# A DFT along the features as seven block products instead of eight

## The chip, the core and the metric

The kernel runs on one NeuronCore of a Trainium2 chip. A core has TensorE (PE in the profile; PEld is its weight load), VectorE (DVE), ScalarE (ACT), GpSimdE (POOL) and SyncE (SP, which here issues the DMAs). Each engine takes its instructions in the order in which the program lists them, and they wait for each other through semaphores. The metric is the device time of one execution in microseconds (us), the median of several runs.

## The reference

Input x is 2048 rows (tokens) by 512 features, and four sublayers run one after the other: A, B, A, B, each with a residual.

```python
def A(x, Ws_re, Ws_im, Wd_re, Wd_im):        # x is a layernorm of the running sum
    a = x @ Wd_re.T                          # DFT along the 512 features
    b = x @ Wd_im.T
    return Ws_re @ a - Ws_im @ b             # DFT along the 2048 tokens, real part

def B(x, w1, w2, w3, w4):                    # 512 -> 512 -> 512, then 512 -> 1376 -> 512
    x1 = x + shifts(gelu(layernorm(x) @ w1)) @ w2
    return x1 + gelu(layernorm(x1) @ w3) @ w4

x = x + A(layernorm(x)); x = x + B(layernorm(x)); x = x + A(layernorm(x)); x = x + B(layernorm(x))
```

One A and the B behind it are called a layer: layer 0 and layer 1. The kernel forms A the other way round: first both token transforms of the normed x, which give a real part (`re`) and an imaginary part (`im`), then the two feature transforms, which it adds.

## The kernel before, in words

**Precision.** A float32 operand is split in two: its rounded high part, made by ScalarE with a copy, and the low rest, made by VectorE with a subtraction. `mm3` (line 294) then issues three matmuls for one product: high by high, high by low, low by high. PE work is therefore counted in threes.

**Chunks and phases.** An A sublayer goes through four chunks of 512 output tokens. A chunk has two phases. `x_phase` (line 499) has 16 half steps, here called s0 to s15: an even one multiplies into the PSUM pairs PC and PB (12 matmuls of 128x512), an odd one into PA (6 matmuls). `y_phase` (line 528) has 16 half steps of 12 matmuls each, here y0 to y15, into PC with PD and into PB with PA. Behind the y phase VectorE puts the sums together in the tiles `re0`, `re1`, `im0`, `im1` (two 128-row blocks each of re and im), and they are split by `high` (ScalarE, line 449) and `low` (VectorE, line 452).

**Feature transforms.** Those of a chunk c are `hid` calls (line 577). For chunks 0 to 2 they are put into the x phase of the chunk behind, eight calls of 12 matmuls of 128x512 at the half steps that `HAT` (line 39) names, into the two PSUM banks PD, four calls for each half of the chunk's tokens. `add_y` (line 593) then adds PD to the rows held in X0 or X1 and sums the rows in the same instruction. For chunk 3 they follow its y phase by themselves.

**What feeds PE.** Every half step and every `hid` call takes one slot of `ring`, four buffers of 1 MB. The slots are filled in a fixed list of items: SyncE loads the raw matrix into one of the `raw` buffers, `stage_one` (line 228) takes differences on VectorE where an item needs them and makes the high part on ScalarE, `stage_two` (line 252) makes the low part on VectorE. `stream()` (line 283) is called once for each item, before its matmuls. It counts the slot of the item before as given back, and lets `prefetch` (line 270) issue `stage_one` of the item three places ahead and `stage_two` of the item two places ahead. An item X so reuses the slot of the item four places before it, and its filling waits until PE has finished with that item. An even half step has an item of the kind "plain" (ScalarE copies 1024 elements a partition, VectorE subtracts 1024), an odd one of the kind "one" (VectorE subtracts 512, ScalarE copies 512, VectorE subtracts 512), a y half step one of the kind "by1" or "by0" (VectorE 1024, ScalarE 1024, VectorE 1024).

**Order by hand.** `late` maps a half step's number to functions; `run_late(i)` runs them right behind that half step's `stream()`, ahead of its matmuls. Nothing reorders the instructions afterwards, so each engine meets them in the order of the code. `hook(i)` behind it issues loads and stores of rows (`rows`, line 204), by SyncE.

**The rest.** The B sublayer (`by_pairs`, line 752) handles chunks in two pairs. In layer 0 the second pair is a loop of five turns (line 1066), then a tail of 11 steps with work of the next layer in `next_steps` (line 986).

Of the kernel before, what the change touches and what calls it, by code (L numbers as in the profile page):

```python
# [40 lines left out]
HORDER = ((1, 0), (0, 1), (1, 1), (0, 0))  # L41


@with_exitstack
def spectral_mlp_kernel(ctx: ExitStack, tc: tile.TileContext, x, ws, hs, w1, w2, w34, out):
# [8 lines left out]
    junk = const.tile([P, D], mybir.dt.bfloat16, name="junk")  # L54
# [10 lines left out]
    w4d = [dram.tile([P, 2, CH], F32, name=f"w4d{i}") for i in range(NF)]  # L65

# [96 lines left out]
    for layer in range(LAYERS):  # L163
        for c in range(NC):
            if layer == 0 and c == 0:
                for k in range(NP):
                    item("plain", piece(ws[c, k][:, 2:4]))
                    item("plain", piece(ws[c, k][:, 0:2]))
                continue
            for k in range(NP):  # L170
                if c:
# [19 lines left out]
    for n, it in enumerate(items):  # L191
        for i in it[1]:
# [3 lines left out]
    state = {"wide": False, "dma": 0, "one": 0, "two": 0, "use": 0, "made": 0, "done": 0, "limit": 0, "load": w_pieces[0]}  # L196
# [11 lines left out]
    def issue_dma(upto=None):  # L208
        while state["dma"] < (state["load"] if upto is None else upto):
# [4 lines left out]
                if (r < RAW or state["wide"] and i in y_pieces)  # L214
# [12 lines left out]

    def stage_one():
# [8 lines left out]
        slots[n] = dest  # L237
        r = [raws[i] for i in ids]
# [13 lines left out]
    def stage_two():  # L252
        n = state["two"]
        kind, ids, (a, b), _ = items[n]
        dest = slots[n]
# [189 lines left out]
    re0s, re1s, im0s, im1s = (f[:, :, 1] for _, f in (re0, re1, im0, im1))  # L445
    mid = [rr[i // 2][i % 2].rearrange("p t r (h d) -> p (t r h) d", h=2) for i in range(4)]
# [52 lines left out]
    def x_phase(c, hook):  # L499
        h = 0  # L500
        for k in range(NP):
            first, last = k == 0, k == NP - 1
            while c and h < NP and HAT[h] == k:
# [12 lines left out]
            if last:  # L516
                for i in range(2):
                    nc.scalar.copy(im1s[:, i], PC[i])  # L518
# [9 lines left out]
    def y_phase(c, hook):  # L528
        for k, kind in y_order():
            first, last = k == 0, k == NP - 1  # L530
            s = stream()
            if kind == "by1":
                hook(k)
                if k == 1:
                    run_late("y")
                if k == 3:
# [5 lines left out]
                if last:  # L542
# [7 lines left out]
                    high(im0)  # L550
            else:
                if k == NP - 2:
# [6 lines left out]
        for i in range(2):  # L559
            nc.scalar.copy(t[:, 2 + i], PA[i])  # L560
        late.update(
# [190 lines left out]
    def by_pairs(layer, zs, xin, dst):  # L752
# [291 lines left out]
        bg += [lows("t4"), *early]  # L1044
        bk, acc1 = mm4, acc4
# [20 lines left out]
        for p in range(NF // 2):  # L1066
# [19 lines left out]
            for f, h in tiles:  # L1086
# [14 lines left out]
            one()  # L1101

        then = next_steps()
        while bg:
            one()

# [577 lines left out]
    for layer in range(LAYERS):  # L1684
        xin = x if layer == 0 else x2d
        last_layer = last_of(layer)
        state["limit"] = w_items[layer]
        zs = {}
        for c in range(NC):
# [90 lines left out]
            def hook(i):  # L1780
# [8 lines left out]
                if i == (13 if layer == 0 and c else 11):  # L1789
                    state["wide"] = True  # L1790
                if c == 0:
# [19 lines left out]
                if i == 4:  # L1811
# [3 lines left out]
                if i == 9:  # L1815
# [3 lines left out]
                if c == NC - 1 and i == 12:  # L1819
                    for j in (0, 1):  # L1820
                        normed_act(tmp[:, j], xt(j), ln2[j])

            x_phase(c, hook)

            def hook(k):
                if layer == 0:
                    prepare_at(c, 2 * NP + k)
                if layer and c == 0:
                    for step, f in zip((1, 1, 2), (ay_sums, ay_highs, ay_lows)):
                        if k == step:  # L1830
                            f(7)
                if k == 1 and c:
                    rows(X1, x1d, (c - 1) * TC + 2, 2, False)
                if c == NC - 1 and k < 2:
                    for q in (2 * k, 2 * k + 1):
                        turn_one(turned0, q, tmp[:, q])
                    for j in (2, 3)[: 2 - 2 * k]:
                        normed_act(tmp[:, j], xt(j), ln2[j])
                if c == NC - 1 and k == 2:
                    turn_out(turned0)  # L1840
# [3 lines left out]
            y_phase(c, hook)  # L1844
# [85 lines left out]
```

## Time and profile before

| what | value |
|---|---|
| median of 3 runs | 1418.96 us (1418.96 to 1420.74) |
| the profiled execution's own time | 1418.97 us |
| its span, first to last instruction | 1417.2 us |
| PE busy | 1409.0 us (99%) |
| VectorE busy | 1191.3 us (84%) |
| ScalarE busy | 765.5 us (54%) |
| all DMA queues | 316.18 MB, mean 223 GB/s |
| granted TensorE clock | 1.000 |

How to read it: the profile is of one execution, and the time around its span is 1.8 us. Busy time counts an instruction from its start to its end, and neighbours on one engine overlap a little, so what an instruction costs an engine that is full is the distance from one start to the next. A row of the timeline has the start, the duration, engine, line, operation, the tiles written and read, and in brackets the idle time before it and what ended it.

### The profile page before, as it was taken

The page shows a single profiled execution, that of the slowest core. Times are in us where ns is not written, and L with a number is a line of the kernel's source. Part 1 is how long each engine was busy: PE and PEld are TensorE (multiplying, and loading weights), DVE is VectorE, ACT ScalarE, POOL GpSimd, SP SyncE. Part 2 cuts the span into 40 slices and gives each one's busy share as a digit, 9 for nine tenths or more (in the row PEclk, how much of TensorE's full clock was granted, in tenths as well). Part 3 has the DMA queues.
Part 4 walks back from the last instruction along what each step waited for, and adds up shares of the span by engine and source line. Part 5 has one row for each costly group of instructions (what it writes and reads, how often), then busy time and mean ns, then how long its engine had stood idle before and what let it go on. Part 6 is the DMA issues. An engine that isn't in the chain of part 4 may idle for free.

```text
span 1417.2 us, 18479 instructions
## 1 busy us (share of the span) xinstructions
PE 1409.0 (99%) x6669; PEld 1181.8 (83%) x6669; DVE 1191.3 (84%) x1684; ACT 765.5 (54%) x1072; POOL 68.2 (5%) x105
## 2 busy tenths in 40 slices
PE   9999999999999999999999999999999999999998
PEld 8888788888788888988888888888888888899887
DVE  7988998998988789956789979879889788897776
ACT  6664555556566655534555545645555566454351
POOL 2100000000001100000000000000000020000000
PEclk9999999999999999999999999999999999999999
DMA  8978858778774748865556476565587457687864
GB/s 290 306 236 302 268 194 274 241 230 309 255 228 146 253 165 264 257 247 180 195 177 218 136 225 206 166 220 170 193 265 237 134 141 245 188 250 252 297 205 160
DMA packets 158907, 316.18 MB, mean 223 GB/s; under 512 B 10848, under 2 KB 78816, under 8 KB 156896
## 3 DMA queue, kind: packets, MB, share of 16 engines
q1 hardware_dynamic: 158816, 315.01, 67.9%
q8 instruction: 52, 0.85, 0.2%
q14 instruction: 39, 0.32, 0.1%
HBM read 260.70 MB, written 54.26 MB: 222 GB/s over the span
## 4 chain that ended last, share of the span: by engine, by line
PE 94%; DVE 3%; DMA 1%; ACT 1%; issue 1%; SPq 0%; POOL 0%; DVEq 0%; ACTq 0%; POOLq 0%
PE psd L295 10%; PE psd L296 10%; PE psd L297 10%; PE psa L295 8%; PE psa L297 8%; PE psa L296 8%; PE psb L296 7%; PE psb L297 7%; PE psb L295 7%; PE psc L295 6%; PE psc L296 6%; PE psc L297 6%; DMA raw<-in_ws 1%; DVE ring L258 1%; DVE rest L492 0%
## 5 line engine op out<-in xcount | busy, mean ns | idle before, releaser
L241 ACT CAST ring<-raw 128x1024 fp32r<-128x1024 f32 x127 | 132.9, 1052 | 69.4 <-PE psd L297 30.6
L258 DVE TENSOR_TENSOR ring<-raw,ring 128x1024 fp32r<-128x1024 f32 x126 | 153.4, 1220 | 14.3 <-ACT ring L241 14.3
L295 PE MATMUL psd<-ring,rr 128*128 128x512 f32 x208 | 80.9, 389 | 0.0
L296 PE MATMUL psd<-ring,rr 128*128 128x512 f32 x208 | 80.9, 389 | 0.0
L297 PE MATMUL psd<-ring,rr 128*128 128x512 f32 x208 | 80.9, 389 | 0.0
L248 ACT CAST ring<-ring0f 128x1024 fp32r<-128x1024 f32 x28 | 29.5, 1054 | 46.9 <-DVE ring0f L247 46.9
L258 DVE TENSOR_TENSOR ring<-ring1f,ring 128x512 fp32r<-128x512 f32 (+1 forms) x56 | 53.3, 952 | 0.8 <-ACT ring L244 0.7
L346 POOL TENSOR_TENSOR rows<-ve,mhalf 128x4 f32<-128x4 f32 x16 | 18.2, 1136 | 735.2 <-DVE ve L345 735.2
L295 PE MATMUL psc<-ring,ay 128*128 128x512 f32 x128 | 50.0, 391 | 1.6 <-ACT rr11f L518 1.6
L296 PE MATMUL psb<-ring,ay 128*128 128x512 f32 x128 | 50.0, 391 | 1.2 <-DVE ring L258 1.2
L297 PE MATMUL psb<-ring,ay 128*128 128x512 f32 x128 | 49.8, 389 | 0.0
L295 PE MATMUL psb<-ring,ay 128*128 128x512 f32 x128 | 49.8, 389 | 0.0
L296 PE MATMUL psc<-ring,ay 128*128 128x512 f32 x128 | 49.8, 389 | 0.0
L297 PE MATMUL psc<-ring,ay 128*128 128x512 f32 x128 | 49.8, 389 | 0.0
L297 PE MATMUL psa<-ring,ay 128*128 128x512 f32 x126 | 49.0, 389 | 0.0
L295 PE MATMUL psa<-ring,ay 128*128 128x512 f32 x126 | 49.0, 389 | 0.0
L295 PE MATMUL psd<-ring,ay 128*128 128x512 f32 x126 | 49.0, 389 | 0.0
L296 PE MATMUL psd<-ring,ay 128*128 128x512 f32 x126 | 49.0, 389 | 0.0
L296 PE MATMUL psa<-ring,ay 128*128 128x512 f32 x126 | 49.0, 389 | 0.0
L297 PE MATMUL psd<-ring,ay 128*128 128x512 f32 x126 | 49.0, 389 | 0.0
L314 POOL TENSOR_TENSOR rs<-ve,mhalf 128x2 f32<-128x2 f32 (+2 forms) x33 | 28.5, 863 | 412.4 <-DVE nb L313 393.4
L697 DVE TENSOR_TENSOR rg<-gt,rg 128x512 fp32r<-128x512 f32 x32 | 22.1, 690 | 29.6 <-ACT rg L696 29.6
(834 smaller groups left out, 4617.1 us busy)
## 6 DMA issues: line engine op xcount, KB each, us to landing
raw<-in_ws SPq DMA_DIRECT2D x183, 512.0 KB, 5.4
raw<-in_hs SPq DMA_DIRECT2D x56, 512.0 KB, 3.7
w3b<-w3d SPq DMA_DIRECT2D x11, 1792.0 KB, 8.5
w4r<-w4d SPq DMA_DIRECT2D x22, 512.0 KB, 3.5
un<-w4s SPq DMA_DIRECT2D x40, 256.0 KB, 3.7
un<-w4d SPq DMA_DIRECT2D x38, 256.0 KB, 4.4
x1d<-tmp SPq DMA_DIRECT2D x12, 512.0 KB, 6.8
xs<-x1d SPq DMA_DIRECT2D x12, 512.0 KB, 5.2
```

Of the source, the lines that this page charges most:

```text
L241: nc.scalar.copy(dest[:, a:b, 0], r[0][:, a:b])
L248: nc.scalar.copy(dest[:, :, 0], lo)
L258: nc.vector.tensor_tensor(lo, src, hi.bitcast(F32), op=ALU.subtract)
L295: nc.tensor.matmul(o, lh, rh, start=first, stop=False, skip_group_check=more)
L296: nc.tensor.matmul(o, lh, rl, start=False, stop=False, skip_group_check=more)
L297: nc.tensor.matmul(o, ll, rh, start=False, stop=last, skip_group_check=more)
L314: nc.gpsimd.tensor_tensor(rs[:, :n], ve[:, :n], mhalf[:, 0, :n], op=ALU.pow)
L346: nc.gpsimd.tensor_tensor(rs, ve, mhalf[:, :, :2], op=ALU.pow)
L697: nc.vector.tensor_tensor(lo, src, hi.bitcast(F32), op=ALU.subtract)
```

## The change

In layer 1, the feature transforms of chunks 0, 1 and 2 are done by a scheme of seven block products in place of eight (Strassen's, in Winograd's form). The left matrix is the chunk's [re; im], cut into four blocks of 256 tokens by 512: a11 and a21 are re, a12 and a22 are im. The right matrix is the pair of DFT matrices, cut in the same way. There are seven left forms (four blocks and sums of them) and seven right forms. A product (`form_product`) takes 24 matmuls of 128x256, and its sums stay in a PSUM bank, onto which later products are added; a drain adds the bank to a half of X0 or X1 after each.

- **Right forms** are made once, in layer 0's second pair: eight units, each 128 columns of the four blocks (`right_load`: two DMAs; `right_sums`: four subtractions of 128 columns on VectorE and copies of seven on ScalarE; `right_keep`: subtractions of seven on VectorE and two or three DMAs to the DRAM tensor `hfd`). Units 0 to 4 go into the five turns of the loop, 5 to 7 into the tail.
- **In the list of items** a product's item has the kind "ready": one DMA of 1 MB from `hfd` straight into the ring's slot, and no work on ScalarE or VectorE. The eight `hid` items of a chunk go.
- **Left forms** replace the splits of im0, re1, im1, re0: seven ScalarE copies and seven VectorE subtractions of 1024, and five further VectorE sums of 1024. The split of im0 leaves the y phase.
- **Row sums**, which `add_y` gave with the addition, are now four ScalarE activations.
- One of four raw buffers is taken for a left form from y half steps k = 5 until half step 14. Some row loads, stores and transposes of chunk 3 move.

`FORMS` gives, for a half step, the product that goes ahead of it, and `DRAINS`, for a product, the half step whose `run_late` drains it. When P3 and P4 are drained, the rows of X0 and X1 are complete and are summed and squared on ScalarE. With P2 for product 2 and so on, the x phase of chunks 1 to 3 in layer 1 now runs: s0 s1 s2 s3 s4 **P2** s5 s6 **P1** s7 **P5** s8 s9 **P6** s10 **P3** s11 **P7** s12 s13 **P4** s14 s15. Bank PD[1] holds P2, P5, P3 (P3 added onto P5), bank PD[0] holds P1, P6, P7, P4, each added onto the last.

```diff
+FORMS = {5: 2, 7: 1, 8: 5, 10: 6, 11: 3, 12: 7, 14: 4}
+DRAINS = {2: 7, 1: 9, 5: 10, 6: 11, 7: 13, 3: 13, 4: 15}
+RIGHT = (1, 6, 2, 3, 5, 7, 4)
...
-                item("plain", p)
-                item("one", p, span=(0, 1))
+                for i, kind in enumerate(("plain", "one")):
+                    if c and layer and 2 * k + i in FORMS:
+                        item("ready", FORMS[2 * k + i])
+                    item(kind, p, span=(0, 2 - i))
...
     def stage_one():
+        if kind == "ready":
+            to = in_forms(dest).rearrange("p u h w -> p (u h w)")
+            nc.sync.dma_start(to.bitcast(F32), hfd[RIGHT.index(ids[0])].rearrange("p u h w -> p (u h w)"))
+            state["one"] += 1
+            return
...
     def x_phase(c, hook, seven=False):
+            if seven and 2 * k in FORMS:
+                form_product(c - 1, FORMS[2 * k])
-            while c and h < NP and HAT[h] == k:
+            while c and not seven and h < NP and HAT[h] == k:
...
+            if seven and 2 * k + 1 in FORMS:
+                form_product(c - 1, FORMS[2 * k + 1])
             s = stream()
             run_late(2 * k + 1)
...
+    def form_product(c, n):
+        s = in_forms(stream())
+        hi, lo, _ = left_forms[n]
+        bank = PD[n in (2, 5, 3)]
+        new = n in (1, 2, 5)
+        for u in range(4):
+            for q in range(2):
+                v = slice(q * P, (q + 1) * P)
+                first = new and u == 0 and q == 0
+                o = bank[:, q * 2 * P : (q + 1) * 2 * P]
+                mm3(o, hi[:, u, v], lo[:, u, v], s[:, u, 0], s[:, u, 1], first, True, not first)
...
+        late.setdefault(DRAINS[n], []).append(
+            lambda: add(x[:, :, cols], bank.rearrange("p (q w) -> p q w", q=2), x[:, :, cols])
+        )
+        if n in (3, 4):
...
+                (14 if n == 3 else "y", row_sums),
+                (15 if n == 3 else "y2", lambda: squares(known, [x[:, 0], x[:, 1]])),
...
     def y_phase(c, hook, seven=False):
+                    if not seven:
+                        high(im0)
...
+        if seven:
+            late.update(
+                {
+                    1: [lambda: add(im1s, im1s, re1s, ALU.subtract), lambda: add(im1s, im1s, X1)],
+                    2: [left_sum("12-22"), left_high(2)],
+                    3: [left_low(2), lambda: add(re1s, re1s, t[:, 0:2])],
+                    4: [lambda: add(re0s, re0s, t[:, 0:2]), lambda: add(re0s, re0s, t[:, 2:4]), left_high(1)],
+                    5: [left_sum(7), left_sum(5)],
+                    6: [left_low(1), left_high(5)],
+                    7: [left_low(5), left_sum(6), left_high(6)],
+                    8: [left_sum(3), left_low(6), left_high(7)],
+                    9: [left_low(7), left_high(3)],
+                    10: [left_low(3), left_high(4)],
+                    11: [left_low(4)],
+                }
+            )
+            return
...
+                if i == 0:
+                    right_sums(p)
+                else:
+                    right_keep(p)
...
+            if not p:
+                right_keep(p)
+            if p < NF // 2 - 1:
+                right_load(p + 1)
...
+        for n, (f, u) in zip((0, 1, 4, 5, 6, 7, 7, 10, 11), ((right_load, 5), (right_load, 6), (right_sums, 5),
+            (right_keep, 5), (right_sums, 6), (right_keep, 6), (right_load, 7), (right_sums, 7), (right_keep, 7))):
+            then[n].append(do((f, u)))
...
-                if i == 4:
+                if i == (3 if layer else 4):
                     rows(X1, xin, j + 2, 2, True)
                 if i == 5:
                     rows(X0, xin, j, 2, True)
-                if i == 9:
+                if i == (15 if layer else 9):
                     rows(X0, x1d, j, 2, False)
```

More of the change, by code (lines that the diff above doesn't have):

```diff
@@ L53, in spectral_mlp_kernel @@
     mhalf = const.tile([P, 2, TC], F32, name="mhalf")
-    junk = const.tile([P, D], mybir.dt.bfloat16, name="junk")
+    junk32 = const.tile([P, 2, P], F32, name="junk")
+    junk = junk32.rearrange("p a b -> p (a b)").bitcast(mybir.dt.bfloat16)
     nc.gpsimd.memset(mhalf, -0.5)
@@ L65, in spectral_mlp_kernel @@
     w4d = [dram.tile([P, 2, CH], F32, name=f"w4d{i}") for i in range(NF)]
+    hfd = dram.tile([7, P, 4, 2, 2 * P], F32, name="hfd")
     ZW = KD * 2 * CH + 32
@@ L170, in spectral_mlp_kernel @@
             for k in range(NP):
-                if c:
+                if c and not layer:
                     for h in range(NP):
@@ L195, in spectral_mlp_kernel @@
     held = {i: None for i in range(len(raw_at))}
-    state = {"wide": False, "dma": 0, "one": 0, "two": 0, "use": 0, "made": 0, "done": 0, "limit": 0, "load": w_pieces[0]}
+    state = {"wide": False, "kept": 0, "dma": 0, "one": 0, "two": 0, "use": 0, "made": 0, "done": 0, "limit": 0, "load": w_pieces[0]}
     x_left = [(0, 1), (1, 1)] + [(j, 2) for j in range(2, NT, 2)]
@@ L254, in stage_two @@
         kind, ids, (a, b), _ = items[n]
+        if kind == "ready":
+            state["two"] += 1
+            return
         dest = slots[n]
@@ L445, in spectral_mlp_kernel, with name_blocks @@
     re0s, re1s, im0s, im1s = (f[:, :, 1] for _, f in (re0, re1, im0, im1))
+    re_im = [both(f"all{i}", RR + i * 8 * CH, KD, 2, CH) for i in range(2)]
+    apart = re0, re1, im0, im1
+    together = [[t[:, 2 * h : 2 * h + 2] for t in pair] for pair in re_im for h in range(2)]
+    def name_blocks(blocks):
+        nonlocal re0, re1, im0, im1, re0s, re1s, im0s, im1s
+        re0, re1, im0, im1 = blocks
+        re0s, re1s, im0s, im1s = (f[:, :, 1] for _, f in blocks)
     mid = [rr[i // 2][i % 2].rearrange("p t r (h d) -> p (t r h) d", h=2) for i in range(4)]
@@ L497, in run_late, with x_phase @@
                 f()
[L499 removed]
+    def x_phase(c, hook, seven=False):
         h = 0
@@ new lines, in left_high, with left_low, left_sum @@
+    def left_high(n):
+        hi, _, src = left_forms[n]
+        return lambda: nc.scalar.copy(hi, src)
+    def left_low(n):
+        hi, lo, src = left_forms[n]
+        return lambda: nc.vector.tensor_tensor(lo, src, hi.bitcast(F32), op=ALU.subtract)
+    def left_sum(n):
+        f = {i: v[2] for i, v in left_forms.items()}
+        o, a, b, op = {
+            7: (f[7], f[1], f[5], ALU.subtract),
+            6: (f[6], f[4], f[7], ALU.subtract),
+            "12-22": (f[3], f[2], f[4], ALU.subtract),
+            3: (f[3], f[3], f[7], ALU.add),
+            5: (f[5], f[5], f[4], ALU.add),
+        }[n]
+        return lambda: add(o, a, b, op)
@@ L529, in y_phase @@
+    def y_phase(c, hook, seven=False):
         for k, kind in y_order():
@@ L549, in y_phase @@
                         nc.scalar.copy(X1[:, i], PD[i])
-                    high(im0)
+                    if not seven:
+                        high(im0)
             else:
-                if k == NP - 2:
+                if k == NP - 2 and not seven:
                     low(im0)
@@ L1788, in hook @@
                         xp_lows(NP - 1, False)
-                if i == (13 if layer == 0 and c else 11):
+                if i == (13 if c else 11):
                     state["wide"] = True
+                if i == 14:
+                    state["kept"] = 0
+                    if layer and c == NC - 1:
+                        name_blocks(apart)
                 if c == 0:
@@ L1819, in hook @@
                 if c == NC - 1 and i == 12:
-                    for j in (0, 1):
+                    for j in (2, 3) if layer else (0, 1):
                         normed_act(tmp[:, j], xt(j), ln2[j])
-            x_phase(c, hook)
+            x_phase(c, hook, layer and c)
             def hook(k):
```

99 lines of the change are left out of this document (87 added, 12 removed).

## The prediction

> **What bounds the kernel now.** I read the head of the page first, then who PE waited for, then the stretches of layer 1's chunks.
>
> ```profile
> PE 1409.0 (99%) x6669; PEld 1181.8 (83%) x6669; DVE 1191.3 (84%) x1684; ACT 765.5 (54%) x1072; POOL 68.2 (5%) x105
> ```
> ```profile
> PE psc L295 <- ACT rr11f L518: 1.6, 2, 0.8
> PE psd L140 <- POOL ident masks.py:199: 1.4, 1, 1.4
> PE psb L296 <- DVE ring L258: 1.2, 1, 1.2
> ```
> ```profile
> core 0: us, PE busy (x) PEld busy (x) DVE busy (x) ACT busy (x) POOL busy (x), PEclk, DMA share, GB/s
> 895.40:949.80 54.40, 54.40 (x241) 45.05 (x241) 43.30 (x53) 27.26 (x34) 1.21 (x2) 1.00 0.63 201
> 949.80:993.20 43.40, 43.40 (x193) 35.92 (x193) 39.76 (x39) 24.01 (x31) 1.34 (x2) 1.00 0.57 184
> ```
>
> PE never rests for long: its three waits add up to 4.2 us of 1417.2. The last two rows are chunk 2's x and y phase in layer 1: PE busy throughout, VectorE 80% and 92%. So time can only come out by PE work taken away, and VectorE is the engine next in line. The first wait also shows that PE waits for a PSUM bank until its sums have been copied out.
>
> PE's price is the distance between starts:
>
> ```profile
> 884.80 0.39 PE L297 MATMUL psc<-ring,ay 128*128 128x512 f32 x1
> ...
> 895.23 0.39 PE L295 MATMUL psc<-ring,ax 128*128 128x512 f32 x1
> ...
> 1299.74 0.28 PE L295 MATMUL psc<-un,hr 128*128 128x256 f32 x1
> ...
> 1304.95 0.28 PE L296 MATMUL psc<-un,hr 128*128 128x256 f32 x1
> ```
>
> The first two are 46 matmuls apart, the last two 46 as well: 10.43/46 = 0.2267 us for 512 columns, 5.21/46 = 0.1133 for 256. Half the columns cost half the time, though each still loads its weights. An even half step is so 12 x 0.2267 = 2.72 us, an odd one 1.36, a `hid` call 2.72, a product 24 x 0.1133 = 2.72.
>
> **What is removed.** Eight `hid` calls become seven products: 21.76 - 19.04 = 2.72 us a chunk, 8.2 us for three. That is the whole gain to be had, because the other engines' savings end no wait.
>
> [...] The measured distances are exactly 2:1, so no fixed part shows here.
>
> **What is added on VectorE, and when.** These rows are chunk 2's x phase, which begins at 895.23:
>
> ```profile
> 895.43 0.69 DVE L243 TENSOR_TENSOR ring3f<-raw 128x512 f32<-128x512 f32 x1 [1.32 <-PE psa L297]
> 896.04 1.22 DVE L258 TENSOR_TENSOR ring<-raw,ring 128x1024 fp32r<-128x1024 f32 x1
> 897.17 0.68 DVE L258 TENSOR_TENSOR ring<-ring3f,ring 128x512 fp32r<-128x512 f32 x1
> 897.78 1.22 DVE L492 TENSOR_TENSOR rr11f<-rr11f,rr01f 128x1024 f32<-128x1024 f32 x1
> 902.23 0.69 DVE L243 TENSOR_TENSOR ring2f<-raw 128x512 f32<-128x512 f32 x1 [0.59 <-PE psb L297]
> ...
> 926.71 0.69 DVE L243 TENSOR_TENSOR ring1f<-raw 128x512 f32<-128x512 f32 x1 [1.03 <-PE psa L297]
> ```
> ```profile
> L492 DVE TENSOR_TENSOR rest<-rest,psd 128x512 f32<-128x512 f32 x21 | 14.4, 686 | 6.2 <-PE psd L297 4.7 <-issue 1.1
> L450 ACT CAST rr<-rr00f 128x1024 fp32r<-128x1024 f32 x8 | 8.4, 1054 | 20.2 <-DVE rr00f L492 20.2
> ```
>
> Three things. Prices: 1.13 us from start to start for 1024 elements (call it A), 0.61 for 512 (B); a drain reads 512 from PSUM, by the L492 row no dearer, so B. Order: slot fillings, then `late` work, as in the code. And the wait: the subtraction for an odd half step (L243) stands until PE has finished the item four places back. At 902.23 it filled s5's slot, which s2 had: s2 ends at 895.23 + 2 x 2.72 + 1.36 = 902.03, and the row starts 0.20 later. It writes only the half that s2's first six matmuls read, yet waits for the last six. VectorE's queue stands with it.
>
> On average VectorE fits: eight low parts (9.1) and four `add_y` (2.7) go from 43.3; four more low parts (4.5), five sums (5.7) and seven drains (4.3) come, 46 in 51.7. But a product added onto a bank, or opening it anew, waits for the drain of the one before, and the drain sits behind such a wait. Step by step, in us from a product's start:
>
> - **P5** reuses P2's bank, drained at half step 7. Between P1 and P5 VectorE's queue reads: s9's subtraction (it takes P1's slot), s8's low part, form 5's low part, sum 6, drain of P2. It stands until P1 is done at 2.72 + 0.20, then needs B + 3A + B = 4.61: P5 starts at 7.6 with 0.1 for the last end and the semaphore. P1 and s7 are over at 4.08. **PE stands 3.6.**
> - **P7** adds onto P6, drained at step 11. Queue: s13's subtraction (P3's slot), s12's low, form 4's low, drain of P6: 2.92 + B + 2A + B = 6.4, +0.1, against 4.08. **2.4.**
> - **P4** adds onto P7, drained at step 13 behind P3's. Queue: s15's subtraction (s12's slot; s12 ends 5.44 after P7's start), s14's low, two drains: 5.64 + 3B + A = 8.6, +0.1, against 6.8. **1.9.**
> - **P1** needs form 1, a block of re0 and re1, which take three sums first. From the phase's start to form 1's low part the queue holds 3 A and 6 B of slot work, eight sums and two low parts: 13 A + 6 B = 18.4. It begins at 0.2, and it stands up to 0.6 more where form 2's low part waits for its high part (1.05 on ScalarE, by the L450 row, if that one waits for the sum that reads the same tile). Form 1 is ready at 18.7 to 19.3; P1's place is at 17.7. **1.5** (1.0 to 1.6).
> - P2 (form 2 done by 9.5, place 10.9), P6 (drain of P1 6.3 after P5's start, place 6.8) and P3 stand for nothing; cover gone, each costs what VectorE is late.
> - **y0** takes PC and PD. ScalarE has P3's row sums ahead of the copies of PC, and P4's drain is late in VectorE's queue:
>
> ```profile
> L337 ACT ACTIVATE junk<-tmp,rows 128x512 bf16<-128x512 f32 x24 | 17.3, 722 | 5.9 <-DVE rows L335 5.2
> L337 ACT ACTIVATION_READ_ACCUMULATOR junk<-tmp,rows 128x1 f32 x24 | 4.5, 187 | 0.0
> ```
>
> Two row sums take 2 x 0.9 = 1.8 in front of the copies; half is covered by the odd half step s15 (1.36). **0.6** (0 to 1.5).
>
> Sum: 3.6 + 2.4 + 1.9 + 1.5 + 0.6 = 10.0 a chunk; less 2.72 it is +7.3, for three chunks **+21.9**.
>
> **DMAs.** A "ready" item waits on SyncE for the slot, so its 1 MB has the three items between: 2.72 + 1.36 + 2.72 = 6.8 us.
>
> ```profile
> w3b<-w3d SPq DMA_DIRECT2D x6, 1024.0 KB, 5.7
> rt<-xtd SPq DMA_DIRECT2D x2, 1024.0 KB, 10.0
> zd<-turned SPq DMA_DIRECT2D x16, 256.0 KB, 5.8
> ```
>
> At 5.7 it lands in time, at 10.0 it would be 3.2 late. The row nearest in kind is the first (whole rows of 8 KB, the DMA share 0.63), and the stalls above widen the windows of P5, P7 and P4; so nothing, upper bound 2 a chunk. Behind a waiting "ready" SyncE holds the raw loads and the row loads at half steps 3 and 5, which have over 10 us. Moved on SyncE's queue are the store of X0 (half step 9 to 15; X0 is not written again before the next y phase has ended) and, for chunk 3, the store of the transposed rows, from k = 2 of the y phase to k = 5, 10.9 ahead of the load that reads them at k = 7:
>
> ```profile
> zt0f<-zd SPq DMA_DIRECT2D x4, 1024.0 KB, 6.7
> ```
>
> Stores of 5.8 end in time; the load lands 38.1 + 6.7 = 44.8 into the phase, and the first to read it is ScalarE behind the first 24 matmuls that follow the phase's 43.5, at 49. No cost, with 4 us to spare.
>
> **Right forms in layer 0.** A unit adds to VectorE four subtractions of 128 columns and 896 of low part; to SyncE 128 KB loads and stores in runs of 512 bytes.
>
> ```profile
> 640.00:655.00 15.00, 15.00 (x68) 12.43 (x67) 9.47 (x18) 6.65 (x11) 0.89 (x2) 1.00 0.55 197
> 700.00:720.00 20.00, 20.00 (x90) 16.57 (x89) 14.55 (x26) 10.86 (x16) 2.04 (x4) 1.00 0.76 259
> 750.00:760.00 10.00, 10.00 (x46) 8.25 (x45) 10.00 (x11) 7.99 (x11) 0.00 (x0) 1.00 0.73 221
> L492 DVE TENSOR_TENSOR sumaf<-sumaf 128x256 f32<-128x256 f32 x6 | 2.6, 426 | 0.2
> ```
>
> With at most 0.43 for a subtraction and 1.1 for the low parts, a unit is below 2.8 us, nearer 2. A turn of the loop (15 us) leaves 5.5 free: no cost. The stores (some 0.9 MB; four of 256 KB in the same runs land in about 6) and the next load fit a turn. The last three units put 6 us into the 5.5 free of the tail, and layer 1 begins with VectorE full (10.00 of 10). I take +1, bounds 0 and 4.
>
> Total: 1418.97 + 21.9 + 1 = **1441.9**, say 1442. The profiled execution stands at the median of the runs (1418.96), so no correction.
>
> **Rivals.**
>
> 1. *The slot comes free by halves.* If the subtraction waited only for the matmuls that read its part of the slot, P5, P7 and P4 would each start 1.36 earlier: stalls 2.2 + 1.1 + 0.6 + 1.5 + 0.6 = 6.0, net +3.3 a chunk, 1418.97 + 9.9 + 1 = 1430. The row at 902.23 speaks against it.
> 2. *Faster.* The drains do not sit behind the subtractions: were each issued right behind its product, VectorE would do it in PE's next half step. It decides at P5: if drain 2 is out before P1 ends, the three large stalls go and 2.1 a chunk remain, mostly hidden by 2.72: 1418.97 - 8.2 + 3 x 0 to 2.1, +1 = 1411 to 1418. For it: the average load of 46 in 51.7. Against: the rows above follow the code's order without exception.
> 3. *The clock falls.* PE stands 3.6 us three times. If the granted clock halved for as long behind each, 3 x 1.8 or more comes on top: 1447 to 1452. The trace grants 1.00 throughout, but its longest wait is 1.4. [...]
>
> That the change doesn't do what it says I exclude: the items, the products and the drains use one table.
>
> **How the numbers follow.** Forecast 0.72, rival 1 0.10, rival 2 0.10, rival 3 0.05, something between that cancels out 0.03. The forecast's own range is 1437 to 1450 (P1 and y0 at their ends give 3 x 8.3 and 3 x 6.2, layer 0 is 0 to 4, late DMAs up to 6, not all at once). With rival 1 and rival 3 the range is 1428 to 1452. A measurement of this kernel tells 0.2% (2.8 us) from no change. Faster 0.10, same 0.03, slower 0.87.
>
> **What would show it.** Right: PE's waits name VectorE's drains (they write X0 and X1, which the profile calls tmp) ahead of psd matmuls, nine of them, of 1.9, 2.4 and 3.6 us; x phases of 61 us for 54.4; 256-column matmuls 0.113 apart. Wrong: no PE wait in the x phases, or waits for a DMA of `hfd`, or for ScalarE in the main; a clock below 1.00 would speak for rival 3, P5 waits near 2.2 for rival 1.

## The result and the profile after

The changed kernel takes **1470.56 us** (median of four runs, 1462.46 to 1471.38); the kernel before, beside it, 1418.96. The ratio is 1.035 (95% interval 1.031 to 1.039): slower, and 28.6 us more than the 1442 forecast. The profiled execution took 1470.83 us, with a span of 1469.0, and is read against the 1417.2 of before: +51.8. The fastest of the four had a granted clock of 0.994, the others 0.986 or 0.987; as 0.007 of 1470 us is 10 us, the 8 us or more between them can be the clock's alone (an estimate).

The head of the page, with the rows of PE's busy tenths and of the granted clock in 40 slices:

```profile
PE 1427.4 (97%) x6885; PEld 1201.7 (82%) x6885; DVE 1211.6 (82%) x1726; ACT 762.1 (52%) x1094; POOL 69.8 (5%) x105
...
PE   9999999999999999999899889889889999999999
...
PEclk9999999999999999999899999999999999999999
```

PE's row has four dips: slice 20 in layer 0's tail, and 23 and 24, 26 and 27, 29 and 30, one for each of layer 1's chunks with products. The clock row shows one dip, in slice 20; a slice is 36.7 us long and a 9 is anything from 0.90, so it hides what shorter windows show below. Who PE waited for (us in total, times, longest):

```profile
PE psd L313 <- DVE tmp L519: 22.6, 10, 3.5
PE psd L313 <- DMA w4r<-w4d: 6.1, 2, 3.6
PE psd L315 <- DVE all L580: 3.6, 3, 1.2
```

The first row is PE waiting for drains (`tmp` is X0 and X1), the third P1 waiting for form 1's low part: both forecast. The second, w4's loads in layer 0's tail, was not.

To see where the time went, the execution is cut at the ScalarE copies that end a y phase, here those of chunk 0 and of chunk 3. The time from one such copy to the next chunk's is called a cycle below. First the kernel before, then the changed one:

```profile
795.79 1.06 ACT L558 COPY tmp<-psb 128x512 f32<-128x512 f32 x2
...
1089.55 1.06 ACT L558 COPY beside<-psb 128x512 f32<-128x512 f32 x2
```
```profile
807.21 1.06 ACT L658 COPY tmp<-psb 128x512 f32<-128x512 f32 x2
...
1141.97 1.06 ACT L658 COPY beside<-psb 128x512 f32<-128x512 f32 x2
```

Up to the first copy 11.4 us are lost (layer 0's second pair and the start of layer 1), between the two 334.76 - 293.76 = 41.0, behind the second nothing (-0.6). The forecast had 1 for the first and 21.9 for the second.

Inside chunk 1, the products that waited:

```profile
828.42 0.39 PE L315 MATMUL psd<-ring,all 128*128 128x256 f32 x1 [1.22 <-DVE all L580]
836.14 0.55 PE L313 MATMUL psd<-ring,all 128*128 128x256 f32 x1 [3.45 <-DVE tmp L519]
858.23 0.38 PE L313 MATMUL psd<-ring,form 128*128 128x256 f32 x1 [2.27 <-DVE tmp L519]
868.72 0.39 PE L313 MATMUL psd<-ring,all 128*128 128x256 f32 x1 [1.76 <-DVE tmp L519]
```

These are P1, P5, P7 and P4, and chunks 2 and 3 have the same four numbers. Now the stretches around P5, and around P7 and P4, cut into pieces of 3.41 us where the trace has the clock change (columns as in the prediction's windows: PE, PEld, DVE, ACT, POOL, granted clock, DMA share, GB/s):

```profile
832.01:835.42 3.41, 0.68 (x3) 0.21 (x2) 3.41 (x5) 0.62 (x1) 0.00 (x0) 1.00 0.29 99
835.42:838.84 3.42, 2.70 (x13) 2.73 (x14) 3.42 (x5) 1.04 (x1) 0.00 (x0) 0.50 0.91 335
838.84:842.25 3.41, 3.41 (x15) 3.22 (x15) 0.63 (x2) 1.89 (x2) 0.00 (x0) 0.50 0.07 29
842.25:845.66 3.41, 3.41 (x16) 2.81 (x15) 2.41 (x3) 1.06 (x2) 0.00 (x0) 1.00 0.00 0
```
```profile
855.90:859.32 3.42, 1.15 (x10) 1.09 (x10) 2.87 (x4) 0.06 (x1) 0.00 (x0) 1.00 0.50 97
859.32:862.73 3.41, 3.41 (x19) 3.41 (x18) 0.00 (x0) 1.04 (x1) 0.00 (x0) 0.50 0.91 359
862.73:866.14 3.41, 3.41 (x17) 2.80 (x17) 0.50 (x1) 0.00 (x0) 0.00 (x0) 1.00 0.01 5
866.14:869.56 3.42, 1.66 (x11) 1.20 (x10) 3.42 (x5) 0.62 (x1) 0.00 (x0) 1.00 0.29 93
869.56:872.97 3.41, 3.41 (x19) 3.41 (x18) 0.84 (x2) 1.05 (x1) 0.00 (x0) 0.50 0.94 322
872.97:876.38 3.41, 3.41 (x18) 2.86 (x18) 2.63 (x3) 1.69 (x4) 0.00 (x0) 1.00 0.72 255
```

In these rows the clock is 1.00 or 0.50 for whole pieces, never between. Each of the three stretches at half speed stands behind a piece in which PE was busy 0.68, 1.15 or 1.66 of 3.4 us. The one behind P5 lasts two pieces: in its first, PE stood for another 0.72 us. In the others PE counts as busy throughout (3.41 of 3.41), yet the matmuls of P5 start 0.2132 us apart there (836.49 to 841.18 is 22 distances) where the forecast has 0.1133. So such a wait is paid for twice, once standing and then at half speed, by these distances 3.41 x (1 - 0.1133/0.2132) = 1.6 us a piece (an estimate). The page's busy time shows the first only. Behind P4 the clock fell in chunk 1 alone. The same wait in chunk 2 lay within one piece as well:

```profile
978.77:982.18 3.41, 1.65 (x11) 1.15 (x10) 3.41 (x5) 0.62 (x1) 0.00 (x0) 1.00 0.24 65
```

The piece behind it ran at full speed.

In layer 0's tail these are the rows, PE's first and SyncE's behind them:

```profile
715.88 0.70 PE L313 MATMUL psd<-w4r,h 128*128 128x512 f32 x1 [2.48 <-DMA w4r<-w4d]
...
726.82 0.77 PE L313 MATMUL psd<-w4r,h 128*128 128x512 f32 x1 [3.65 <-DMA w4r<-w4d]
```
```profile
708.33 0.98 SPq L1191 DMA_DIRECT2D hfd<-cells  x2
709.40 2.31 SPq L950 DMA_DIRECT2D w4r<-w4d  x2
...
717.43 0.98 SPq L1191 DMA_DIRECT2D hfd<-cells  x2
...
720.95 0.47 SPq L950 DMA_DIRECT2D w4r<-w4d  x1
```

On SyncE the stores of `right_keep` for units 5 and 6 stand until VectorE has made the low parts, and w4's loads come behind them; the second issues 5.9 us before the matmul that waits for it.

So my theory after the result was: VectorE's waits as forecast (9 us a chunk); the clock halved for a window behind a wait that leaves PE idle for half of it; layer 0's tail late by SyncE's queue. The rivals: products of 256 columns slow the clock by themselves; layer 0 costs nothing and everything lies in layer 1; VectorE's time, not the queue, is what layer 0's tail lacks.

### The profile page after: what moved, and what is told of

Read it like the earlier page. It is cut to its first block, busy times and chain, and to the rows that moved or that the text cites. A ratio compares the mean times of both kernels' runs of the same rounds, so it can differ in the third digit from the quotient of the medians.

```text
span 1469.0 us, 19013 instructions
## 1 busy us (share of the span) xinstructions
PE 1427.4 (97%) x6885; PEld 1201.7 (82%) x6885; DVE 1211.6 (82%) x1726; ACT 762.1 (52%) x1094; POOL 69.8 (5%) x105
## 4 chain that ended last, share of the span: by engine, by line
PE 84%; DVE 9%; DMA 2%; ACT 2%; issue 2%; SPq 0%; DVEq 0%; POOL 0%; ACTq 0%; POOLq 0%
PE psd L313 9%; PE psd L315 9%; PE psd L314 9%; PE psa L313 7%; PE psa L315 7%; PE psa L314 7%; PE psb L314 6%; PE psb L315 6%; PE psb L313 6%; PE psc L313 6%; PE psc L314 6%; PE psc L315 6%; DVE ring L276 2%; DVE all L580 1%; DMA raw<-in_ws 1%
## 5 line engine op out<-in xcount | busy, mean ns | idle before, releaser
L256 ACT CAST ring<-raw 128x1024 fp32r<-128x1024 f32 x103 | 107.6, 1050 | 77.1 <-PE psd L315 39.6
L276 DVE TENSOR_TENSOR ring<-raw,ring 128x1024 fp32r<-128x1024 f32 x102 | 124.3, 1220 | 13.0 <-ACT ring L256 12.9
L313 PE MATMUL psd<-ring,all 128*128 128x256 f32 x120 | 38.4, 320 | 15.6 <-DVE tmp L519 15.6
L276 DVE TENSOR_TENSOR ring<-ring1f,ring 128x1024 fp32r<-128x1024 f32 (+1 forms) x50 | 49.2, 984 | 1.7 <-ACT ring L263 0.9
L263 ACT CAST ring<-ring1f 128x1024 fp32r<-128x1024 f32 x28 | 29.5, 1053 | 32.9 <-DVE ring1f L262 32.6
L276 DVE TENSOR_TENSOR ring<-ring3f,ring 128x1024 fp32r<-128x1024 f32 (+1 forms) x44 | 45.1, 1025 | 1.4 <-ACT ring L259 1.1
L263 ACT CAST ring<-ring3f 128x1024 fp32r<-128x1024 f32 x28 | 29.6, 1057 | 29.8 <-DVE ring3f L262 29.8
```

The source lines that it names most:

```text
L256: nc.scalar.copy(dest[:, a:b, 0], r[0][:, a:b])
L263: nc.scalar.copy(dest[:, :, 0], lo)
L276: nc.vector.tensor_tensor(lo, src, hi.bitcast(F32), op=ALU.subtract)
L313: nc.tensor.matmul(o, lh, rh, start=first, stop=False, skip_group_check=more)
```

## The experiments

### The right forms alone

```diff
 (kernel before)
+                if i == 0:
+                    right_sums(p)
+                else:
+                    right_keep(p)
...
+            then[n].append(do((f, u)))
```

Layer 1 is the old one, nobody reads the forms.

> The kernel before with nothing but layer 0's right forms added (the eight units are summed, split and stored, and nobody reads them); layer 1 keeps its eight calls a chunk. My theory: layer 0's second pair pays about 11 us, because SyncE's queue stands at the stores of units 5 and 6 while VectorE still works, w4 loads are queued behind them, and PE waits for those; so 1427 to 1433 us, with rows of PE waiting for w4r in the tail. Rival: all of the loss sits in layer 1 and the right forms cost what the prediction said (0 to 4 us): 1419 to 1423 us.

Measured: 1430.89 us, ratio 1.0084 (1.0067 to 1.0101). The end of chunk 0's y phase came at 807.02, as late as in the changed kernel, and two waits for w4r stood in the tail:

```profile
716.63 0.47 PE L297 MATMUL psd<-w4r,h 128*128 128x512 f32 x1 [1.98 <-DMA w4r<-w4d]
...
727.45 0.77 PE L297 MATMUL psd<-w4r,h 128*128 128x512 f32 x1 [5.12 <-DMA w4r<-w4d]
```

The right forms in layer 0 cost 11.6 us, not 0 to 4; the other 40 of the 51.6 are layer 1's.

### Gaps in the kernel before

```diff
                     add_y(c - 1, h // 4, PD, ...)
+                    if h < 4:
+                        for i in range(EXTRA.pop(0)):     # 4, 5, 6, 7, 8, 9
+                            add(X0[:, 1], X0[:, 1], PD[1], ALU.subtract)
+                            add(X0[:, 1], PD[1], X0[:, 1])
```

> The kernel before with useless VectorE pairs (subtract PD[1] from X0, add it again: 4, 5, 6, 7, 8, 9 pairs of 2 x 0.61 us for chunks 1 to 3 of layer 0 and of layer 1) behind the first addition, so that the fifth feature call waits for its bank: six gaps of about 2 to 9 us, behind which only matmuls of 512 columns run. Theory 1 (the clock falls behind a gap of some 2 us already, whatever the matmuls are): behind gaps of 1.7 us and more the next call takes 4 to 5 us instead of 2.72, and windows of 10 us behind them show a granted clock of 0.75 to 0.9. Theory 2 (it needs an idle time of over 3.4 us): no loss behind the gaps below 3.4 us, 2 us and more behind those above. Theory 3 (what slows is the products of 256 columns, gaps have no part in it): 2.72 us behind every gap.

Measured, in one run: gaps of 3.41, 5.31, 6.76, 7.75, 9.19 and 10.64 us, and behind every one whole pieces of 3.41 us at a granted clock of 0.50. The matmuls have 512 columns, so the products' shape has no part in it: theory 3 falls. The gaps came out larger than meant, all of 3.4 us or more, so theories 1 and 2 were left undivided. A second run with fewer and shorter pairs, `EXTRA` now listing their columns:

```diff
+EXTRA = [(512, 512, 256), (512,) * 3, (512, 512, 512, 256)] * 2
```

> The kernel before with useless VectorE pairs as in the earlier run, fewer and shorter: gaps ahead of the fifth feature call of about 1.8, 2.4 and 3.3 us in layer 0's chunks 1 to 3 and 1.4, 2.0 and 2.8 us in layer 1's, only matmuls of 512 columns around them. Theory 1 (the clock goes by the share of a window of some 3.4 us in which PE was idle, about half is enough): no loss behind 1.4 us, one stretch of 3.4 us at half the clock (1.7 us lost) behind those of 2.4 us and more, the ones between by chance of where they fall. Theory 2 (it takes 3.4 us without a matmul): no loss behind any.

| gap, us | 1.43 | 1.43 | 1.96 | 2.42 | 2.87 | 3.33 |
|---|---|---|---|---|---|---|
| most of it that lies in one piece of 3.41 us | 1.43 | 1.24 | 1.96 | 2.07 | 2.73 | 2.80 |
| at a granted clock of 0.50 behind it, us | none | none | 3.41 | 3.41 | 3.41 | 3.41 |

A seventh gap, of 1.88 us, came along in layer 0; 1.57 of it lay in one piece, and the clock stayed. The gap of 1.96, cut as above:

```profile
942.66 0.50 PE L297 MATMUL psd<-ring,rr 128*128 128x512 f32 x1 [1.96 <-DVE ring L259]
```
```profile
940.28:943.70 3.42, 1.46 (x6) 0.86 (x5) 3.39 (x5) 0.00 (x0) 0.00 (x0) 0.99 0.13 11
943.70:947.11 3.41, 3.41 (x10) 2.65 (x8) 2.54 (x5) 2.30 (x6) 0.00 (x0) 0.51 0.83 263
947.11:950.52 3.41, 3.41 (x16) 2.82 (x15) 1.37 (x3) 1.58 (x2) 1.01 (x1) 1.00 0.97 341
```

No gap reached 3.4 us, and the clock fell: theory 1 holds, theory 2 falls.

### PE kept busy in the gaps

```diff
+FILL = {7: 15, 11: 10, 13: 8}
             mm_half(PA, ax[k][:, 0], s[:, 0], first, last)
+            if seven:
+                for i in range(FILL.get(2 * k + 1, 0)):
+                    nc.tensor.matmul(PA[i % 2], ax[k][:, 0][:, 0, 0:P], zeros[:, 0:1].to_broadcast([P, D]), start=False, stop=False)
```

> The changed kernel with matmuls of 512 zero columns put where PE waits ahead of P5, P7 and P4 (15, 10 and 8 of 0.227 us, behind half steps 7, 11 and 13, added to PA: zeros, so the sums stay what they are). The waits on VectorE stay as long as they are, but PE does not stand still in them. My theory (the clock falls because PE is idle): P5, P7 and P4 take 2.7 to 2.9 us instead of 4.4 to 5.3, some 4 to 6 us a chunk are back: 1452 to 1461 us. Rival (it falls because of what the products are, or because of a rest counted otherwise than by PE's matmuls): unchanged, 1466 to 1473 us, products behind the gaps still 4 us and more.

Measured: 1458.56 us, ratio 1.0278 (1.0263 to 1.0294), 12.0 less than the changed kernel, although not one of PE's waits for VectorE was mended. Layer 1's three cycles fell from 112.91, 111.24 and 110.61 us to 107.23, 107.25 and 107.61, by 12.7 in sum. P5 took 2.95 us in place of 5.25. The same stretch, first in the changed kernel and then in this one:

```profile
830.00:850.00 20.00, 16.55 (x89) 14.91 (x89) 13.65 (x15) 6.63 (x8) 0.00 (x0) 0.83 0.52 191
```
```profile
830.00:850.00 20.00, 19.82 (x120) 17.59 (x120) 13.65 (x15) 7.56 (x10) 0.00 (x0) 1.00 0.66 236
```

VectorE did the same 13.65 us of work, and the clock stayed at 1.00. The clock's share of the loss behind P5, P7 and P4 is thereby shown: 12 to 13 us in three chunks.

The run shows one thing more, in layer 0's tail, where no zeros were put. A wait longer than P4's left the clock alone; it lay across two pieces, 0.99 us in one and 1.19 in the other:

```profile
716.94 0.47 PE L317 MATMUL psd<-w4r,h 128*128 128x512 f32 x1 [2.18 <-DMA w4r<-w4d]
```
```profile
712.34:715.75 3.41, 2.42 (x11) 1.68 (x9) 1.81 (x6) 1.46 (x2) 0.00 (x0) 1.00 0.99 276
715.75:719.16 3.41, 2.22 (x10) 1.87 (x11) 2.99 (x5) 1.35 (x3) 0.00 (x0) 1.00 0.81 312
719.16:722.58 3.42, 3.42 (x16) 2.56 (x14) 3.39 (x5) 1.48 (x3) 0.00 (x0) 1.00 0.82 235
```

### The drains ahead of the slot fillings

```diff
-DRAINS = {2: 7, 1: 9, 5: 10, 6: 11, 7: 13, 3: 13, 4: 15}
+DRAINS = {2: "6b", 1: 8, 5: 10, 6: 10, 7: 12, 3: 12, 4: 15}
-                    5: [left_sum(7), left_sum(5)],
-                    6: [left_low(1), left_high(5)],
-                    7: [left_low(5), left_sum(6), left_high(6)],
+                    5: [left_sum(7), left_low(1)],
+                    6: [left_sum(5), left_high(5), lambda: run_late("6b"), left_low(5)],
+                    7: [left_sum(6), left_high(6)],
```

The load of X0's rows moves too, from half step 5 to behind P2's `stream()`.

> The changed kernel with the order of layer 1's x phase altered so that every drain comes ahead of the slot filling in VectorE's queue before it is due (P2's drain within half step 6, P1's in 8, P6's in 10, P7's and P3's in 12), with low1 and the sum of form 5 swapped; layer 0 as in the changed kernel. My theory: PE's 26 us of waits for drains go and the clock's loss behind them goes too; what stays is layer 0's 11 us less the 8.2 us gained and some rest of waits: 1422 to 1434 us. Rival A (the clock falls in the products of 256 columns by themselves, not behind gaps): only the waits go, 1470.6 - 26 = 1444 to 1455 us with clock windows still at 0.8 to 0.9 in layer 1. Rival B (the waits come from elsewhere): 1465 to 1472 us.

Measured: 1445.24 us, ratio 1.0183 (1.0167 to 1.0198). By time alone this is rival A's range, but its mark is missing: chunk 2's products ran at full clock.

```profile
922.00:969.00 47.00, 43.71 (x268) 38.24 (x267) 35.82 (x40) 17.55 (x24) 0.00 (x0) 1.00 0.75 252
```

PE's waits in this run:

```profile
PE psd L313 <- DMA w4r<-w4d: 6.3, 2, 4.2
PE psd L313 <- DMA ring<-hfd: 5.1, 6, 1.2
PE psd L313 <- DVE all0f L519: 3.3, 2, 1.7
PE psd L313 <- DVE tmp L519: 2.5, 2, 2.3
```

The drains' 22.6 us became 2.5, and the clock's loss went with them in chunks 1 and 2. In chunk 3 one wait for a drain, of 2.30 us, is left, with 3.41 us at half speed behind it. What my sum lacked is the second row: with PE no longer standing, the 6.8 us between two uses of a slot are too short for a product's megabyte, which took 6.7 us from issue to landing (median). It also lacked the third: P1 waits, 1.6 to 1.7 us in each chunk, until form 5's sum is done, which is written into the same tile as form 1. The cycles were 101.7, 101.2 and 106.7 us against 97.92 before.

### Products later, and a load in two halves

```diff
-FORMS = {5: 2, 7: 1, 8: 5, 10: 6, 11: 3, 12: 7, 14: 4}
+FORMS = {6: 2, 8: 1, 9: 5, 10: 6, 11: 3, 12: 7, 14: 4}
+DRAINS = {2: 7, 1: 9, 5: 10, 6: 10, 7: 12, 3: 12, 4: "15-"}   # "15-" runs ahead of s15's stream()
```

Both runs also have the tail described below under "stores later".

> The mended tail, and in layer 1 the products P2, P1, P5 half a step or a step later (FORMS = {6: 2, 8: 1, 9: 5, 10: 6, 11: 3, 12: 7, 14: 4}), the drains early (DRAINS = {2: 7, 1: 9, 5: 10, 6: 10, 7: 12, 3: 12, 4: '15-'}, the last ahead of s15's stream) and the left forms' order to match. My theory: PE's waits for VectorE and the clock's losses in layer 1 go; what stays is 0.15 us a product, 2 to 3 us of DMA waits a chunk and 1 to 3 us in layer 0: 1419 - 8.2 + 3.2 + 3 x 2 + 2 = 1422 us, 1417 to 1427. Rival (VectorE has no room for the forms wherever the products stand, so that another wait of some 2 us a chunk comes in the place of each one mended): 1432 to 1445 us.

Measured: 1450.00 us, ratio 1.0218 (1.0201 to 1.0235). Neither my 1422 nor the rival's mechanism: PE waited 16.0 us for `ring<-hfd` in 8 pieces of up to 3.7, and the clock fell behind two of them. The longest of each chunk were P1's: in chunk 1 its load was issued at 824.53, behind a raw load that SyncE issued only at 823.23, and it landed at 832.3, just ahead of P1's start at 832.55.

```diff
-            nc.sync.dma_start(to.bitcast(F32), hfd[...])
+            for half in (slice(0, 8 * P), slice(8 * P, 16 * P)):
+                nc.sync.dma_start(to[:, half].bitcast(F32), src[:, half])
```

> The same with the 1 MB load of each ready item cut into two DMAs of 0.5 MB, so that a product can start when its first half is there. If what stays is PE waiting for the whole megabyte: 3 to 6 us less than without the cut, 1414 to 1420 us, and waits for ring<-hfd under 0.3 us. If both halves land together (they share the same DMA engines): no difference, within 1.5 us of the run without.

Measured: 1445.22 us, ratio 1.0187 (1.0171 to 1.0202): 4.8 less than without the cut, as forecast for the difference; but 9.1 us of waits for `hfd` stay, and the time itself is 25 over the upper end of what I had put.

### GpSimdE for the units, then for the loads

Products still later (`FORMS = {7: 2, 8: 1, 9: 5, ...}`, `DRAINS` 2 at 8), one DMA an item.

```diff
-                add(x[:, o], x[:, a], x[:, b], ALU.subtract)
+                nc.gpsimd.tensor_tensor(x[:, o], x[:, a], x[:, b], op=ALU.subtract)
```

> As the run with later products and one DMA an item, with two changes: the right forms' sums and subtractions are done by GpSimdE in place of VectorE (all eight units), and P2, P1, P5 stand at FORMS = {7: 2, 8: 1, 9: 5, ...}, so that three items with 6.8 us of matmuls lie between the freeing of each product's slot and the product. Theory: what was left in layer 0 after its stores were moved is VectorE's time (about 2 us a unit, in the way of drains and slot fillings), and GpSimdE takes it off: layer 0's loss falls from about 11 to 2 to 4 us; layer 1 keeps DMA waits behind raw loads in SyncE's queue, 3 to 6 us a chunk: 1428 to 1440 us. Rival: GpSimdE is so slow at these, or so much in VectorE's way, that stores and next loads come later: layer 0's loss stays at 10 us or more, 1440 us and above.

Measured: 1458.78 us, ratio 1.0274 (1.0259 to 1.0289). The rival is right: chunk 0 ended at 811.7, 4.5 later than in the changed kernel, and PE waited for ScalarE's `h` three times, up to 1.6 us, as it does nowhere in the changed kernel. ScalarE's copies of a unit stand behind GpSimdE's sums, up to 6.1 us. GpSimdE took 2.11 us for a 128x896 subtraction, twice the 1.08 us of VectorE in the changed kernel:

```profile
L1195 POOL TENSOR_TENSOR cells<-cells 128x896 fp32r<-128x896 f32 x3 | 6.3, 2111 | 5.9 <-ACT cells L1186 5.9
```

```diff
-            nc.sync.dma_start(to.bitcast(F32), hfd[...])
+            nc.gpsimd.dma_start(to.bitcast(F32), hfd[...])
```

> The same with the ready items' DMAs issued by GpSimdE's queue in place of SyncE's, where they stand behind loads of raw matrices that wait for a buffer. Theory: the DMA waits ahead of products (up to 3.7 us, 16 us in all) come from that queue and go: 8 to 14 us less than with SyncE's queue, 1416 to 1428 us. Rival: they come from the transfer itself (1 MB beside the other loads takes 6 to 7 us whoever issues it): within 3 us of the run with SyncE's queue.

Measured: 1462.62 us, ratio 1.0306 (1.0289 to 1.0323), 3.8 more than with SyncE's queue. The queue had its part in the DMA waits: they fell from 13.8 to 3.3 us, P1's load in chunk 1 was issued at 824.57 in place of 829.99, and a load landed 5.4 us behind its issue in place of 7.0 (medians). But no time came of it: in their place PE waited 14.0 us for VectorE (`DVE tmp L519`, three times, up to 4.7), P5 for P2's drain. With the products packed between s6 and s11, VectorE is late again.

### Layer 0's tail: stores later

```diff
-            (0, 1, 4, 5, 6, 7, 7, 10, 11),
+            (0, 1, 4, 5, 6, 7, 7, 9, 10, 12),
-                (right_keep, 5),
+                (right_lows, 5),
...
+                (right_store, 5),
+                (right_store, 6),
```

> The changed kernel with right_keep cut in two in layer 0's tail, subtractions (right_lows) and stores (right_store), and the stores of units 5 to 7 issued later, when VectorE has long done them; layer 1 as in the changed kernel. My theory (SyncE's queue stood at the stores and w4's loads behind them): the two waits for w4r go with the clock's loss behind them, 8 to 11 us less than the changed kernel: 1459 to 1463 us, w4r waits under 1 us. Rival (w4 lands late because the stores take the DMA engines' time, whatever their order of issue): waits for w4r of 4 us and more stay, 1467 to 1472 us.

Measured: 1466.91 us, ratio 1.0345 (1.0327 to 1.0363). That is 3.65 less than the changed kernel, and not clear of its spread (1462.46 to 1471.38). The waits for w4r are gone to the last, so the queue was what they came from; but the time did not follow. Two others stand there now:

```profile
730.75 0.47 PE L313 MATMUL psa<-ring,ax 128*128 128x512 f32 x1 [2.45 <-DVE xs L1073]
...
738.60 0.50 PE L314 MATMUL psc<-ring,ax 128*128 128x512 f32 x1 [1.74 <-DVE ring L276]
```

The first is my own doing: VectorE stood 1.78 us for unit 7's load, ahead of the pair's last drain. The second is a slot filled late, and 3.41 us at half speed follow it. To divide order from load, two runs on the kernel before: the loop's five units alone, and all eight with unit 7's work behind the last drain.

```diff
 (kernel before with the right forms)
-        for n, (f, u) in zip(
...
-            then[n].append(do((f, u)))
```

> The kernel before with the right forms of units 0 to 4 only, those in the loop of five turns; units 5 to 7 are left out, and nobody reads the forms. My theory: the loop has room (VectorE 61.05 us of 80 before), its units cost one wait of 1.3 us, and the loss is the tail's: 1419 to 1422 us. Rival: every unit costs its 1.4 us wherever it stands, 5/8 of 11.6 = 7 us: 1425 to 1428 us.

Measured: 1420.71 us, ratio 1.0013 (1.0004 to 1.0022): the loop's units cost 2 us, with one new wait of 1.26. The tail's three cost the other 10.

```diff
 (kernel before with the right forms, stores later as above)
-                (right_sums, 7),
         drain(c2, acc2)
+        right_sums(7)
+        right_keep(7)
```

> The kernel before with all eight units, the stores of 5 and 6 issued later, and unit 7's sums, subtractions and store put behind the last drain of the tail. Theory A (what cost was the order: SyncE's queue standing at the stores ahead of w4's loads, VectorE standing at unit 7's load ahead of a drain): no PE wait above 1.3 us in the tail, 1420 to 1424 us. Theory B (VectorE has no 2 us to spare for each of the three units between 700 and 760 us, whatever the order): new waits for slot fillings or drains of 2 to 5 us in sum with the clock's loss behind them, 1425 to 1430 us.

Measured: 1429.06 us, ratio 1.0072 (1.0057 to 1.0087), 1.8 less than with the first order. No wait for w4r, none for a drain; in their place these:

```profile
720.68 0.50 PE L297 MATMUL psd<-w4r,h 128*128 128x512 f32 x1 [1.08 <-ACT h L665]
734.28 0.51 PE L297 MATMUL psa<-ring,ax 128*128 128x512 f32 x1 [0.78 <-ACT ring L246]
738.76 0.50 PE L298 MATMUL psc<-ring,ax 128*128 128x512 f32 x1 [1.74 <-DVE ring L260]
748.38 0.50 PE L298 MATMUL psc<-ring,ax 128*128 128x512 f32 x1 [1.02 <-DVE ring L260]
```

The time and the waits are theory B's, though no piece at half speed stands behind these. My theory of SyncE's queue was the smaller part of it: with the stores later, in both orders that I tried (unit 7 ahead of the last drain and behind it), VectorE, and ScalarE with it, had no room for three units there, and the order chose which wait showed it. That no order has room is not shown.

### All mends together

```diff
 (changed kernel, drains ahead of the slot fillings, the tail of the run above)
-DRAINS = {2: "6b", 1: 8, 5: 10, 6: 10, 7: 12, 3: 12, 4: 15}
+DRAINS = {2: "6b", 1: 8, 5: 10, 6: 10, 7: 12, 3: 12, 4: "15-"}
...
+            for half in (slice(0, 8 * P), slice(8 * P, 16 * P)):
```

> The changed kernel with the products where it has them, the early drains, P4's drain ahead of s15's stream, the two half DMAs for a ready item and the tail of the run just described. Sum: 1419 - 8.2 + 3.2 (0.15 us a product) + 3 x 3.5 (P1's wait of 1.7, rests of DMA waits, start of y) + 3 (layer 0) = 1427 us, 1421 to 1433. Under 1418 would say that the seven products can win with the right order; over 1435 that one mend still brings another wait.

Measured: 1436.43 us, ratio 1.0124 (1.0107 to 1.0141), granted clock 0.999. Layer 1's three cycles are 100.15, 99.74 and 101.10 us, 7.2 over the kernel before in sum, where I had put 5.5; layer 0 is 9.7 late where I had put 3. So no order that I tried came under the kernel before. No piece at half speed is left in layer 1, and one in layer 0's tail. What is left in layer 1's chunks is P1's 1.7 us, rests of DMA waits (1.8 us in sum), the start of the y phase, and the price of the products themselves.

## Why the prediction was wrong

The direction and VectorE's mechanism were right. Three terms of the sum were not: the clock, put at nothing; layer 0, put at +1; and a product's price.

**Right: the waits.** Forecast 3.6, 2.4, 1.9, 1.5 and 0.6 us for P5, P7, P4, P1 and y0; measured in chunk 1, as idle time, 3.45, 2.27, 1.76, 1.22 and 0.18: 8.9 for 10.0. Counted from start to start, as the forecast counts, the first three are 3.61, 2.43 and 1.92, and all waits of the three chunks 29.3 us for 30.0. So writing VectorE's queue out by start to start distances priced the waits. Rivals 1 and 2 (the slot by halves, drains early) are excluded by the same rows.

**Right: DMAs at nothing**, under a condition that I named: PE's stalls widen the windows. In the runs that took stalls away, the loads became waits of 1.8 to 16.0 us in sum.

**Wrong: the clock as a rival at 0.05, "3 x 1.8 or more".** It should have been a term of the sum. The trace of the kernel before could not show it, since its longest wait is 1.4 us, and behind waits of 1.43 us the clock stayed (the run with short gaps). That the chance was so low rested on no trace: I took it that PE must do nothing for a whole window. The runs show that a window with PE busy for 1.15 or 1.46 of 3.41 us is enough, and one with 1.65 sometimes (P4's in chunk 1, not in chunk 2). So not three waits had to be priced but up to nine, of which seven were followed by half speed in the profiled execution, and layer 0's as well. Measured by the filled gaps: 12.0 us between the medians, 12.7 between layer 1's cycles.

**Wrong: "the last three units put 6 us into the 5.5 free of the tail ... I take +1, bounds 0 and 4".** Measured 11.6 for the eight units, 10 of them for these three. The term read free time off an average. With the stores out of the way, PE waited there for a drain and for slot fillings, so the free time was not where the work fell. A unit is a chain (VectorE, ScalarE, VectorE) in which each engine waits for the other, and its stores stood on SyncE ahead of w4's loads, a queue at which the term did not look. How the 10 us divide among these is not shown. The five units in the loop cost 2, near the nothing that was forecast.

**Mis-sized: a product at 2.72 us.** These rows of the run with early drains are 22 matmuls apart:

```profile
922.42 0.28 PE L314 MATMUL psd<-ring,all 128*128 128x256 f32 x1
...
925.05 0.28 PE L315 MATMUL psd<-ring,all 128*128 128x256 f32 x1
```

2.63/22 = 0.1195 us, not the 0.1133 of `un,hr`, so 24 of them take 2.87. Seven products cost 1.05 us a chunk more, so the gain to be had was 1.7 a chunk and not 2.72. Why they are slower I did not test.

**The sum again.** By the distances from start to start of PE's matmuls in the profiled execution, each less the 0.2267 or 0.1133 us that the forecast gives it, layer 1 is: -8.2 + 29.3 (waits) + 13.4 (matmuls at half speed) + 3.9 (matmuls of products at full speed) + 2.2 (pieces at other matmuls, the starts of the y phases among them) = 40.6 of the 41.0 measured. Layer 0: 11.4, of which 2 are the loop's.

## What to carry to other kernels

A wait of PE can have a second price: in these runs, when PE was idle for 1.92 us or more of a window of 3.41 us, the next window ran at half clock. So count 1.6 us more (the estimate above) for a wait that puts about 2 us into one window (2.3 behind P5's wait of 3.45: P5 took 5.25 us, and 2.95 with the gaps filled), and look for it in windows of a few us, since the page's slices hide it. A kernel whose PE is 99% busy has no free time to be read off averages: work put beside it must be placed against the queue of every engine that it touches, SyncE's too. And a mend must be judged by the time, not by the wait that it removes: three times here (the early drains, GpSimdE's queue, the later stores) the wait named by the profile went and others took its place.

## What the runs showed of the hardware

- The granted clock was 1.00 or 0.50 for whole windows of 3.41 us on one grid. In the changed kernel half speed begins at 715.95, 726.18, 835.41, 859.30, 869.54, 948.05, 971.94, 1060.69 and 1081.17, always whole multiples of 3.413 us apart.
- What decided in these traces was PE's idle time within one window. In the 15 traces of this case, all 41 full-speed windows with 1.92 us of it or more were followed by one at half speed (in the changed kernel 8 of them, with 2.27 to 3.02 us), and none of the 74 with 1.0 to 1.73 us; of the 12 between, 5 were. A wait of 2.18 us that lay across two windows, 0.99 and 1.19, left the clock alone (the run with zeros), and the same 1.76 us within one window lowered it in the changed kernel's chunk 1 and not in its chunk 2.
- A half-speed window with 0.64 us of idle time or more was followed by another one (19 of 19; in the changed kernel 3, with 0.64, 0.73 and 1.00), one with 0.54 or less by full speed (46 of 46).
- Keeping PE on matmuls by zeros through a gap held the clock at 1.00 (window 830 to 850 us; 0.83 in the changed kernel, without them).
- At full speed matmuls of 256 columns ran 0.1195 us apart in the products (the run with early drains; 0.120 in the changed kernel) and 0.1133 elsewhere (`un,hr`, in the kernel before and in the changed one). At half speed those of the products ran 0.2132 apart.
- 1 MB loads landed 5.4 us behind their issue when GpSimdE issued them and 7.0 when SyncE did (medians of 21), in kernels that differ in this alone. They are issued at other times as well, and which of the two makes the landing shorter is not shown.
